# One attention and expert kernel: part of the feature map and the row scaling go to GpSimd, masks are added by quarters of the array, and the first x is transposed at other units

## The chip, the cores and the metric

The kernel runs on 1 core of one Trainium2 chip. The metric is device time in microseconds of one execution. Engines are named as in the profile: PE is TensorE (PEld its weight loads), DVE is VectorE, ACT is ScalarE, POOL is GpSimd, SP is SyncE, which issues the DMAs.

## What is computed

Three layers follow one another: attention with a memory over 4 batches and 8 heads of 576 tokens with 64 features, then a dense gated layer over the 2304 tokens, then a layer of 8 experts of which each token takes one. The change touches the first, and the normalization ahead of the second:

```python
scores = np.where(causal, -1000000000.0, scale * (q @ k.T))
a = np.exp(scores - scores.max(-1)); a /= a.sum(-1) + 1e-09
local = a @ v
phi = lambda x: np.where(x > 0, x, np.exp(x) - 1.0) + 1.0
mem_out = (phi(q) @ M_prev) / (phi(q) @ z_prev + 1e-06)
x = g * mem_out + (1 - g) * local            # 2304 tokens x 512
xn = x / np.sqrt(np.mean(x * x, -1) + 1e-06) * rms_g
y = (silu(xn @ w_gate) * (xn @ w_val)) @ w_out
```

## The kernel before

**Attention.** Two batches lie on the two halves of the 128 partitions, so one pass serves a head of both: 16 passes, called heads here. A head is five units (`ORDER`): four `Pair`s of two query tiles each, with 128, 384, 256 and 512 keys, and a `Last` for the 64 tokens left over, with 576 keys. The loop at the end of `attention` runs over 80 units and three more, and is a pipeline written out by hand: at unit u the PE computes the scores of unit u, transposes the weights of unit u-2 and multiplies those of unit u-3 with the values; ACT takes the exponentials in between. Work on the side is written as generators, each of which goes one step further at the end of a unit: `phi` (feature map of q for two heads), `load`, `rms`, the decoder's pieces of the dense weights (float64 to float32), and what `side` adds. In this part the instructions of each engine stand exactly in the order in which the program writes them (`Core.chain`), and every engine works its queue in that order. One unit takes some 2.7 us.

**Feature map** (`phi`, L248 to L261). For `phi` of two heads, one unit after another: min(q, 0) on DVE (L257), the exponential on ACT (L259), then max(q, 0) plus it, in one DVE instruction (L261). `recall` multiplies the result with the memory at the next units.

**Masks** (L336 and L382). A query tile of 64 rows for one batch and the same for the other make 128 rows; the scores come as four matmuls of 64 x 64 quarters of the array, two for each of two tiles. The causal mask is then added by one more matmul for each tile over the whole array, identity times a table of zeros and -1e9 in bf16.

**Scaling** (`rms`, L456). When the 9 tiles of a pair of batches (128 tokens x 512) are ready, ACT sums their squares, one tile a unit; POOL and DVE make y, the inverse root; then DVE multiplies each tile by its y in place (L478) and SP stores it to `xd` in DRAM. The first pair does this in the second half of attention, the other (`late`) in the first dense block.

**First x.** `xload` reads 4 tiles of `xd` back at unit (12, 2), and `xtrans` transposes a quarter of their features at each of the units in `XT` (L36, in the form (head, place in the head)) and splits it into a high and a low part: PE to PSUM (`tp`), ACT (`xh`), DVE (`xl`). The PSUM tile `tp` has the tag `m`, of which there is one buffer; `recall`'s `mp` and the `avl` of each `Last` use the same one. `avl` is written three units after its `Last`, so at units 72 and 77 for the heads 13 and 14.

**Dense layer.** Five blocks of tokens (4, 4, 4, 4 and 2 tiles), each with 12 steps f: gate and value matmuls (`gv`), tanh and products (`th`), and the output matmuls (`acc`) of the step before. Weights are kept as a high and a low part. In the first block ACT, DVE and POOL also make these parts (`Wf`), decode the last 15 pieces of weights (L206 to L219), and work off `late`. Here a scheduler orders each engine's instructions by its own model of time. The low part `sl` of the gated product is subtracted on POOL (L1014).

The expert layer behind it is not touched.

Of the kernel before, what the change touches and what calls it, by code (L numbers as in the profile page):

```python
# [12 lines left out]
AF = mybir.ActivationFunctionType  # L13
ALU = mybir.AluOpType
# [3 lines left out]
P = 128  # L18
# [14 lines left out]
FLATE = 7  # L33
DEC = [round(3 + 3.5 * k) for k in range(3 * FLATE)]
AHEAD = 3
XL, XT = (12, 2), ((14, 0), (14, 2), (14, 4), (15, 1))  # L36
NEARLY = 4
NMAIN = 18
NSLOT = 21
# [182 lines left out]
def attention(ctx, nc, tc, ins, c, g8, rp, ps, xd, side):  # L222
# [10 lines left out]
    def half(t, p):  # L233
        return p ^ (t & 1)

    def rows(p):
        return slice(64 * p, 64 * p + 64)
# [10 lines left out]
    def phi(n):  # L248

        q = pl.tile([P, 2, S], F32, tag='qs', name='q')  # L250
        nc.sync.dma_start(q, qs[n // 4, n % 4].rearrange('b p s -> p b s'))
        ph = pl.tile([P, 2, S], F32, tag='ph', name='ph')
        phis.append(ph)
        yield
        if n:
            yield
        nc.vector.tensor_scalar(ph, q, 0.0, None, op0=ALU.min)  # L257
        yield
        nc.scalar.activation(ph, ph, AF.Exp)  # L259
        yield  # L260
        nc.vector.scalar_tensor_tensor(ph, q, 0.0, ph, op0=ALU.max, op1=ALU.add)  # L261

    def values(n):

# [13 lines left out]
    for _ in load(0):  # L278
        pass
    work = [phi(0), load(1)]  # L280
    for w in work:
        next(w)
# [39 lines left out]
    class Pair:  # L322
# [5 lines left out]
        def score(self):  # L328
            H, i, w = self.H, self.i, self.w
            sc = ps.tile([P, 2, 512], F32, tag='sc', bufs=2, name='sc')  # L330
            for j in range(2):
                for p in range(2):
                    t, r = 2 * i + j, rows(half(j, p))
                    PE.matmul(sc[rows(p), j, :w], H.qt[r, 0, 64 * t:64 * t + 64], H.qt[r, 1, :w], start=True, stop=False)
            for j in range(2):
                PE.matmul(sc[:, j, i * P:w], c['identb'], c['maskb'][:, j], start=False, stop=True)  # L336
            m = sm.tile([P, 2], F32, tag='m', name='m')
            nc.vector.tensor_reduce(m, sc[:, :, :w], axis=AX.X, op=ALU.max, negate=True)
            self.sc, self.m = sc, m
# [28 lines left out]
    class Last:  # L368
# [5 lines left out]
        def score(self):  # L374
            H = self.H
            m = sm.tile([P, 2], F32, tag='m', name='m')
            sc = ps.tile([P, 2, 512], F32, tag='sc', bufs=2, name='scl')
            for u in range(2):
                for p in range(2):
                    r = rows(p)  # L380
                    PE.matmul(sc[r, u, :288], H.qt[r, 0, 512:576], H.qt[r, 1, 288 * u:288 * u + 288], start=True, stop=(u == 0))
            PE.matmul(sc[:, 1, 224:288], c['identb'], c['maskb'][:, 0, :64], start=False, stop=True)  # L382
            mx = sm.tile([P, 2], F32, tag='mx', name='mx')
            nc.vector.tensor_reduce(mx, sc[:, :, :288], axis=AX.X, op=ALU.max, negate=True)
            nc.vector.tensor_tensor(m[:, 0:1], mx[:, 0:1], mx[:, 1:2], op=ALU.min)
            self.sc, self.m = sc, m
# [17 lines left out]
        def value(self):  # L404
            H = self.H
            avl = ps.tile([P, 64], F32, tag='m', name='avl')
            for k in range(5):
                for p in range(2):
                    lt, rhs = (self.aT[:, k], H.v[:, H.h, k, p]) if k < 4 else (self.aT[:64, 4], H.vL[:, H.h, p])
                    PE.matmul(avl[rows(p)], lt[:, rows(p)], rhs, start=(k == 0), stop=(k == 4))  # L410
            add(H, avl)
            if H.hh == 7 and H.bp == 0:
                work.append(rms(0))
# [42 lines left out]
    def rms(bp, ps=None):  # L456

        ts, n = (0, 1, 2, 3, 8, 4, 5, 6, 7), 9
        x = [xs[bp][t // 4][:, t % 4] for t in ts]
        pool = rp if bp else cp  # L460
        ss, y, z = (pool.tile([P, 9], F32, tag=f'{n}{bp}', name=n) for n in ('ss', 'y', 'z'))
        if 'mhalf' not in state:
            state['mhalf'] = rp.tile([P, 9], F32, name='mhalf')
            nc.gpsimd.memset(state['mhalf'], -0.5)
        for t in range(n):
            sq = cp.tile([P, 512], F32, tag='sq', name='sq') if not bp else ps.tile([P, 512], F32, tag='m', name='sq')
            nc.scalar.activation(sq, x[t], AF.Square, accum_out=ss[:, t:t + 1])
            yield
        nc.vector.tensor_scalar(ss, ss, 1.0 / 512, 1e-6, op0=ALU.mult, op1=ALU.add)
        nc.gpsimd.tensor_tensor(y, ss, state['mhalf'], op=ALU.pow)  # L470
        yield
        yield
        nc.vector.tensor_tensor(z, y, y, op=ALU.mult)
        nc.vector.tensor_tensor(z, z, ss, op=ALU.mult)
        nc.vector.tensor_scalar(z, z, -0.5, 1.5, op0=ALU.mult, op1=ALU.add)
        nc.vector.tensor_tensor(y, y, z, op=ALU.mult)
        for j, t in enumerate(ts):
            nc.vector.tensor_scalar(x[j], x[j], y[:, j:j + 1], None, op0=ALU.mult)  # L478
            r = (8 * bp + t if t < 8 else 16 + bp) * P
            nc.sync.dma_start(xd[r:r + P, :], x[j])  # L480
            yield
# [4 lines left out]
    for u in range(5 * 16 + LAG2):  # L486
        n, j = u // 5, u % 5
        if n < 16:
            if j == 0:
                H = start(n)  # L490
            if j == LD and n < 14:
                work.append(load(n + 2))
            if u % 10 == 1 and n < 14:
                work.append(phi(n // 2 + 1))
            if u == 32:
                memory(1)
            if u % 10 == 4 and n < 14:
                values(n // 2 + 1)
            units.append(Last(H) if ORDER[j] == 4 else Pair(H, ORDER[j]))
            units[u].score()  # L500
# [21 lines left out]
    def late(ps):  # L522
        yield from rms(1, ps)
# [586 lines left out]
PE = None  # L1110
# [98 lines left out]
```

## Time and profile before

| | us |
|---|---|
| time, median of 3 runs (lowest to highest) | 1040.76 (1039.47 to 1041.92) |
| the profiled execution's own time | 1039.59 |
| its span, first to last instruction | 1037.9 |
| PE busy in it (mean granted clock 0.991) | 974.7 |
| DVE busy | 696.3 |
| ACT busy | 569.8 |
| POOL busy | 248.8 |

A span is the time from the first to the last instruction of the profiled execution; 1.7 us of that execution lie around it. Attention runs from 0 to about 236 us, the first dense block from there to about 346, the other four to about 730, the experts behind them to the end. An engine's busy share says little by itself; what a change in a stage is worth is read from the waits and the chain there.

### The profile page before, as it was taken

The numbers are of one execution on the slowest core, as the hardware profiler recorded it, in microseconds if no ns is written. First come the engines' busy times: TensorE is split into PE (matmuls) and PEld (weight loads), VectorE is DVE, ScalarE is ACT, GpSimd is POOL, SyncE is SP. The second block draws the span as 40 slices with busy tenths as digits, with TensorE's granted clock in tenths as the row PEclk, the third lists the DMA queues.
The fourth block names the chain that finished last, engine by engine and source line by source line (L and its number), as shares of the span: only waits on it lengthen the run. The fifth ranks groups of instructions, "written<-read, shape, count | busy, mean of one in ns | idle before, by whom it ended". The sixth has DMA issues, their size and how long they took to land.

```text
span 1037.9 us, 18552 instructions
## 1 busy us (share of the span) xinstructions
PE 974.7 (94%) x6727; PEld 752.1 (72%) x6727; DVE 696.3 (67%) x1256; ACT 569.8 (55%) x1113; POOL 248.8 (24%) x241
## 2 busy tenths in 40 slices
PE   7999989799899999999999999999989999999995
PEld 4666656557676768887888778878768888777784
DVE  6788899777986544334422462357688889888884
ACT  6888887766343322222222222244557888888884
POOL 1233243235454311110111112123012121222110
PEclk9999999989999999999999999999999999999999
DMA  9466557315644311121211112144124552396332
GB/s 313 152 206 188 181 168 229 107 62 179 208 131 142 112 31 62 32 73 29 72 32 51 31 63 65 35 162 134 41 83 143 172 197 76 122 339 216 102 112 89
DMA packets 51278, 128.20 MB, mean 124 GB/s; under 512 B 9965, under 2 KB 10477, under 8 KB 50672
## 3 DMA queue, kind: packets, MB, share of 16 engines
q1 hardware_dynamic: 47664, 116.48, 34.9%
q0 software_dynamic: 3520, 10.51, 3.2%
q8 instruction: 54, 0.88, 0.4%
q14 instruction: 40, 0.33, 0.1%
HBM read 160.50 MB, written 22.04 MB: 176 GB/s over the span
## 4 chain that ended last, share of the span: by engine, by line
PE 60%; DVE 14%; issue 8%; DMA 7%; ACT 7%; POOL 2%; SPq 0%; ACTq 0%; POOLq 0%; DVEq 0%
PE gv L56 22%; PE acc L56 11%; PE y L56 9%; PE h L56 7%; DMA out_dram<-ys,to 2%; DVE m L56 2%; PE av L56 2%; PE sc L56 2%; PE tr L56 2%; DMA wo<-woutd 1%; PE tp L56 1%; ACT whl L858 1%; PE htp L56 1%; DVE whl L859 1%; DVE dt L56 1%
## 5 line engine op out<-in xcount | busy, mean ns | idle before, releaser
L56 PE MATMUL gv<-xh,Wf 128*128 128x512 f32 (+1 forms) x960 | 291.2, 376 | 8.9 <-DVE th L1009 3.2
L859 DVE TENSOR_TENSOR whl<-raw,whl 128x1024 fp32r<-128x1024 f32 x173 | 204.3, 1220 | 32.0 <-ACT whl L858 31.6
L56 PEld LDWEIGHTS gv<-xh,Wf 128*128 128x128 f32 x960 | 175.7, 190 | 44.5 <-DVE th L1009 4.8
L858 ACT CAST whl<-raw 128x1024 fp32r<-128x1024 f32 x176 | 177.0, 1059 | 17.2 <-PE h L56 5.1
L56 PE MATMUL gv<-xl,Wf 128*128 128x512 f32 (+1 forms) x480 | 177.6, 370 | 0.0
L1014 POOL TENSOR_TENSOR sl<-th,sh 128x512 fp32r<-128x512 f32 (+1 forms) x58 | 73.0, 1259 | 321.5 <-ACT sh L1013 316.9
L56 PE MATMUL y<-whl,hh 128*128 128x512 f32 x528 | 138.3, 402 | 2.3 <-DVE whl L859 1.5
L56 PE MATMUL h<-whl,xgh 128*128 128x512 f32 x352 | 117.3, 401 | 2.7 <-DVE whl L859 2.0
L56 PEld LDWEIGHTS y<-whl,hh 128*128 128x128 f32 x528 | 97.5, 190 | 23.4 <-DVE whl L859 2.1
L56 PEld LDWEIGHTS gv<-xl,Wf 128*128 128x128 f32 x480 | 91.2, 190 | 14.2
L1013 ACT CAST sh<-th 128x512 fp32r<-128x512 f32 (+1 forms) x60 | 34.5, 576 | 118.9 <-DVE th L1010 118.9
L951 DVE TENSOR_TENSOR wol<-wo,woh 128x512 fp32r<-128x512 f32 x60 | 45.0, 751 | 70.3 <-ACT woh L950 70.3
L56 PE MATMUL acc<-woh,sh 128*128 128x512 f32 x216 | 86.6, 401 | 1.0 <-ACT sh L1013 0.9
L56 PE MATMUL acc<-wol,sh 128*128 128x512 f32 x216 | 85.3, 395 | 0.0
L56 ACT ACTIVATE a<-sc,m 128x128 f32<-128x128 f32 (+3 forms) x128 | 67.0, 534 | 30.5 <-DVE m L56 17.4
L1009 DVE SCALAR_TENSOR_TENSOR th<-th,gv 128x512 f32<-128x512 f32 (+1 forms) x60 | 37.9, 631 | 63.0 <-ACT th L1008 62.7
L56 PEld LDWEIGHTS h<-whl,xgh 128*128 128x128 f32 x352 | 64.6, 188 | 21.2 <-DVE whl L859 7.0
L56 PE MATMUL acc<-woh,sl 128*128 128x512 f32 x216 | 77.7, 397 | 2.2 <-POOL sl L1014 2.2
L1008 ACT ACTIVATE th<-gv 128x512 f32<-128x512 f32 (+1 forms) x60 | 33.2, 554 | 81.0 <-PE gv L56 76.9
L950 ACT CAST woh<-wo 128x512 fp32r<-128x512 f32 x60 | 37.1, 619 | 63.0 <-PE acc L56 43.3
L1010 DVE TENSOR_TENSOR th<-th,gv 128x512 f32<-128x512 f32 (+1 forms) x60 | 37.9, 632 | 49.8 <-PE gv L56 49.2
L56 PE MATMUL h<-whl,xgl 128*128 128x512 f32 x176 | 68.7, 392 | 0.0
(252 smaller groups left out, 1572.8 us busy)
## 6 DMA issues: line engine op xcount, KB each, us to landing
raw<-in_wf_dram SPq DMA_DIRECT2D x168, 512.0 KB
wo<-woutd SPq DMA_DIRECT2D x60, 256.0 KB
raw<-in_wgv_dram SPq DMA_DIRECT2D x24, 512.0 KB
qt<-in_qk_dram SPq DMA_DIRECT2D x16, 576.0 KB
raw<-in_wout_dram SPq DMA_DIRECT2D x12, 512.0 KB
q<-in_qs_dram SPq DMA_DIRECT2D x8, 576.0 KB
xd<-x SPq DMA_DIRECT2D x18, 256.0 KB
rowd<-xr SPq DMA_DIRECT2D x4, 1028.0 KB
```

Of the source, the lines that this page charges most:

```text
L56: i = call(*args, **kw).ins
L858: nc.scalar.copy(w[:, 0], src)
L859: (nc.gpsimd if k in pool_k else nc.vector).tensor_tensor(w[:, 1], src, w[:, 0].bitcast(F32), op=ALU.subtract)
L950: nc.scalar.copy(woh, wo)
L951: nc.vector.tensor_tensor(wol, wo, woh.bitcast(F32), op=ALU.subtract)
L1008: nc.scalar.activation(th, g[0], AF.Tanh, scale=0.5)
L1009: nc.vector.scalar_tensor_tensor(th, th, 1.0, g[0], op0=ALU.add, op1=ALU.mult)
L1010: nc.vector.tensor_tensor(th, th, g[1], op=ALU.mult)
L1013: nc.scalar.copy(sh, th)
L1014: (nc.vector if f >= 10 and bi == last else nc.gpsimd).tensor_tensor(sl, th, sh.bitcast(F32), op=ALU.subtract)
```

## The change

There are four edits. In `phi` the minimum on DVE goes; ACT takes the exponential of q itself, one unit earlier than before; POOL takes max(q, 0) in place, one unit later; DVE then forms min(exp(q), 1) + max(q, 0), where it stood before. In the masks each whole-array matmul becomes two, of the quarters that the scores used. In `rms` the multiplication of a tile by y goes from DVE to POOL. In `XT` the second and the fourth place change.

```diff
--- before.py
+++ after.py
@@ -33,7 +33,7 @@
 FLATE = 7
 DEC = [round(3 + 3.5 * k) for k in range(3 * FLATE)]
 AHEAD = 3
-XL, XT = (12, 2), ((14, 0), (14, 2), (14, 4), (15, 1))
+XL, XT = (12, 2), ((14, 0), (14, 3), (14, 4), (15, 0))
 NEARLY = 4
 NMAIN = 18
 NSLOT = 21
@@ -254,11 +254,11 @@
         yield
         if n:
             yield
-        nc.vector.tensor_scalar(ph, q, 0.0, None, op0=ALU.min)
-        yield
-        nc.scalar.activation(ph, ph, AF.Exp)
-        yield
-        nc.vector.scalar_tensor_tensor(ph, q, 0.0, ph, op0=ALU.max, op1=ALU.add)
+        nc.scalar.activation(ph, q, AF.Exp)
+        yield
+        nc.gpsimd.tensor_scalar(q, q, 0.0, None, op0=ALU.max)
+        yield
+        nc.vector.scalar_tensor_tensor(ph, ph, 1.0, q, op0=ALU.min, op1=ALU.add)
 
     def values(n):
 
@@ -333,7 +333,9 @@
                     t, r = 2 * i + j, rows(half(j, p))
                     PE.matmul(sc[rows(p), j, :w], H.qt[r, 0, 64 * t:64 * t + 64], H.qt[r, 1, :w], start=True, stop=False)
             for j in range(2):
-                PE.matmul(sc[:, j, i * P:w], c['identb'], c['maskb'][:, j], start=False, stop=True)
+                for p in range(2):
+                    r = rows(half(j, p))
+                    PE.matmul(sc[rows(p), j, i * P:w], c['identb'][r, r], c['maskb'][r, j], start=False, stop=True)
             m = sm.tile([P, 2], F32, tag='m', name='m')
             nc.vector.tensor_reduce(m, sc[:, :, :w], axis=AX.X, op=ALU.max, negate=True)
             self.sc, self.m = sc, m
@@ -379,7 +381,9 @@
                 for p in range(2):
                     r = rows(p)
                     PE.matmul(sc[r, u, :288], H.qt[r, 0, 512:576], H.qt[r, 1, 288 * u:288 * u + 288], start=True, stop=(u == 0))
-            PE.matmul(sc[:, 1, 224:288], c['identb'], c['maskb'][:, 0, :64], start=False, stop=True)
+            for p in range(2):
+                r = rows(p)
+                PE.matmul(sc[r, 1, 224:288], c['identb'][r, r], c['maskb'][r, 0, :64], start=False, stop=True)
             mx = sm.tile([P, 2], F32, tag='mx', name='mx')
             nc.vector.tensor_reduce(mx, sc[:, :, :288], axis=AX.X, op=ALU.max, negate=True)
             nc.vector.tensor_tensor(m[:, 0:1], mx[:, 0:1], mx[:, 1:2], op=ALU.min)
@@ -475,7 +479,7 @@
         nc.vector.tensor_scalar(z, z, -0.5, 1.5, op0=ALU.mult, op1=ALU.add)
         nc.vector.tensor_tensor(y, y, z, op=ALU.mult)
         for j, t in enumerate(ts):
-            nc.vector.tensor_scalar(x[j], x[j], y[:, j:j + 1], None, op0=ALU.mult)
+            nc.gpsimd.tensor_scalar(x[j], x[j], y[:, j:j + 1], None, op0=ALU.mult)
             r = (8 * bp + t if t < 8 else 16 + bp) * P
             nc.sync.dma_start(xd[r:r + P, :], x[j])
             yield
```

In the order of the instructions the change shows at three places that matter.

ScalarE around one feature map (here the one for the heads 12 and 13), before; `a` are the softmax weights, `aT` their transposes, `aL` and `scl` those of a `Last`, `ph` the feature map:

```order
L56 COPY aT<-tr 128x384 x2
L56 ACTIVATE a,sums<-sc,m 128x512 x2
L56 COPY aT<-tr 128x2x256
L56 ACTIVATE aL,sums<-scl,m 128x288 x2
L56 ACTIVATE qt<-qt 128x576
L56 ACTIVATE ph<-ph 128x1152
```

and after:

```order
L56 COPY aT<-tr 128x384 x2
L56 ACTIVATE a,sums<-sc,m 128x512 x2
L56 ACTIVATE ph<-q 128x1152
L56 COPY aT<-tr 128x2x256
L56 ACTIVATE aL,sums<-scl,m 128x288 x2
L56 ACTIVATE qt<-qt 128x576
```

The exponential moved ahead of a copy, the weights of the `Last` and the scaling of the next head's q.

TensorE at the second transposition of x, before (`avl` is the product of head 13's `Last` with the values, into the buffer that `tp` takes next):

```order
L56 MATMUL avl<-v,aTL 64x64 x8
L56 MATMUL avl<-vL,aTL 64x64 x2
L56 MATMUL tp<-ident,xt 128x128 x4
L56 MATMUL sc<-qt 64x512 x4
```

and after, where the masks by quarters show as well:

```order
L56 MATMUL avl<-v,aTL 64x64 x8
L56 MATMUL avl<-vL,aTL 64x64 x2
L56 MATMUL sc<-qt 64x512 x4
L56 LDWEIGHTS identb
L56 MATMUL sc<-maskb,identb 64x128
L56 LDWEIGHTS identb
L56 MATMUL sc<-maskb,identb 64x128
L56 LDWEIGHTS identb
L56 MATMUL sc<-maskb,identb 64x128
L56 LDWEIGHTS identb
L56 MATMUL sc<-maskb,identb 64x128
L56 MATMUL tr<-ident,a 128x128 x6
```

A unit's scores, masks, transposes and products now lie between `avl` and `tp`; on the other hand the second, third and fourth `tp` follow one another at a distance of one unit.

GpSimd in the first dense block, before (from `y` of the second pair of batches on; `sl` is the low part of the gated product, `Wf` low parts of weights, `sq` the decoder's last addition):

```order
L56 TENSOR_TENSOR y<-ss,mhalf 128x9
L1014 TENSOR_TENSOR sl<-th,sh 128x512
L211 TENSOR_TENSOR sq<-dt,sq 128x512
L219 TENSOR_TENSOR Wf<-sq,Wf 128x512
L56 TENSOR_TENSOR Wf<-dw,Wf 128x512
L1014 TENSOR_TENSOR sl<-th,sh 128x512
```

and after:

```order
L56 TENSOR_TENSOR y<-ss,mhalf 128x9
L1018 TENSOR_TENSOR sl<-th,sh 128x512
L211 TENSOR_TENSOR sq<-dt,sq 128x512
L56 TENSOR_SCALAR x_1717<-x_1717,y 128x512 x4
L56 TENSOR_SCALAR x_1719<-x_1719,y 128x512
L56 TENSOR_SCALAR x_1718<-x_1718,y 128x512 x4
L219 TENSOR_TENSOR Wf<-sq,Wf 128x512
L56 TENSOR_TENSOR Wf<-dw,Wf 128x512
L211 TENSOR_TENSOR sq<-dt,sq 128x512
L1018 TENSOR_TENSOR sl<-th,sh 128x512
```

All nine scalings stand in one piece ahead of the weights of step 3.

## Rows read from the trace of the kernel before

**Rows 1.** Stretches, core 0: start:end, us, busy us (instructions) per engine, clock, DMA share, GB/s

```profile
0.00:236.00 236.00, 210.48 (x3089) 138.78 (x3089) 191.06 (x402) 178.20 (x522) 69.30 (x108) 0.99 0.56 178
236.00:276.00 40.00, 36.86 (x160) 28.98 (x161) 33.04 (x52) 20.61 (x43) 21.04 (x16) 1.00 0.65 214
346.00:690.00 344.00, 338.87 (x1581) 273.29 (x1580) 136.24 (x310) 92.98 (x163) 53.75 (x44) 1.00 0.18 54
```

**Rows 2.** Chain that ended last: shares by engine and line, 0 to 236 and 236 to 276

```profile
by line: issue 8.7%; DVE m L56 8.5%; PE av L56 8.2%; PE sc L56 7.8%; PE tr L56 7.1%; DVE dt L56 4.4%; ACT a L56 4.4%; PE mp L56 4.1%; ACT aL L56 4.1%; ACT aT L56 3.9%; DVE sq L56 3.8%; DVE tm L56 3.6%; DVE r L56 2.9%; ACT ph L56 2.8%; DMA q
...
by line: DMA dw<-wgvd 18.5%; DMA wo<-woutd 16.8%; DVE x L56 13.1%; DVE Wf L56 10.7%; issue 7.4%; DVE z L56 6.2%; DVE wol L951 5.1%; POOL x L56 4.3%; POOL sl L1014 3.4%; DVE th L1010 3.0%; SPq L196 2.1%; DVE dt L208 2.0%; DVE Wf L219 1.7%; D
```

**Rows 3.** Timeline, TensorE around the x transposes: start us, us, engine, line, instruction

```profile
10.69 1.09 PE L56 MATMUL sc<-qt 64*64 64x512 f32 x8 [0.79 <-ACT a L56]
...
207.87 1.11 PE L56 MATMUL tp<-ident,xt 128*128 128x128 f32 x4 [2.68 <-DVE tm L56]
208.92 1.99 PE L56 MATMUL sc<-qt 64*64 64x512 f32 x8
...
223.89 0.69 PE L56 MATMUL avl<-v,aTL 128*64 128x64 f32 x16 [1.64 <-DVE xl L56]
...
224.78 1.92 PE L56 MATMUL sc<-qt 64*64 64x512 f32 x6
```

**Rows 4.** Stretches of 2 and 1 us after the two waits, columns as in rows 1

```profile
208.00:210.00 2.00, 2.00 (x12) 0.89 (x12) 0.25 (x1) 0.97 (x2) 1.39 (x3) 0.50 0.00 0
225.00:226.00 1.00, 1.00 (x8) 0.01 (x2) 0.93 (x4) 0.89 (x4) 0.00 (x0) 0.50 0.91 352
```

**Rows 5.** Timeline, TensorE: masks and the transposes behind them

```profile
112.01 0.29 PE L56 MATMUL sc<-maskb,identb 128*128 128x128 bf16 x2
112.13 1.04 PE L56 MATMUL tr<-ident,a 128*128 128x128 f32 x8
```

**Rows 6.** Tile ph: duration ns min/median/max, first and last start

```profile
L56 DVE TENSOR_SCALAR ph<-q x8: 746/748/1825, 6.9 to 180.0; 128x1152 f32<-128x1152 f32 x8
```

**Rows 7.** Waits from 0 to 228: us in total, times, longest

```profile
DVE ph L56 <- ACT ph L56: 8.8, 7, 1.9
```

**Rows 8.** Chain in order of time, 92 to 104: start us, us, what

```profile
98.87 1.05 ACT ph L56
```

**Rows 9.** Tile x: the scaling by mean square, duration ns min/median/max

```profile
L56 DVE TENSOR_SCALAR x<-x,y x18: 471/478/1508, 151.1 to 262.6; 128x512 f32<-128x512 f32 x18
```

**Rows 10.** Groups of instructions by line: busy us, mean ns

```profile
L56 POOL MEMSET MZ<- 128x1040 f32 x1 | 1.0, 964 | 0.1
```

**Rows 11.** Tile dt of the decoder: duration ns min/median/max

```profile
L56 DVE TENSOR_SCALAR dt<-sq x21: 412/419/986, 27.3 to 227.3; 128x512 int32<-128x512 int32 x21
L56 DVE SCALAR_TENSOR_TENSOR dt<-raw,dt x21: 672/683/1439, 30.2 to 229.4; 128x512 int32<-128x512 int32 x21
...
L56 POOL TENSOR_TENSOR sq<-dt,sq x21: 1262/1280/1733, 34.9 to 232.3; 128x512 f32<-128x512 f32 x21
```

**Rows 12.** Stretch 0 to 236, instructions that touch dt alone (VectorE, then GpSimd)

```profile
0.00:236.00 236.00, 40.71 (x63) 27.71 (x21) 0.99 0.56 178
```

**Rows 13.** Timeline, 210.3 to 212: a GpSimd and a VectorE instruction side by side

```profile
210.30 1.27 POOL L56 TENSOR_TENSOR Wf<-dw,Wf 128x512 fp32r<-128x512 f32 x1 [0.91 <-ACT Wf L56]
210.41 1.45 DVE L56 TENSOR_SCALAR sq<-dt 128x512 int32<-128x512 int32 x1
```

**Rows 14.** Timeline, first dense block, 257 to 267

```profile
257.03 4.12 DVE L56 TENSOR_SCALAR x<-x,y 128x512 f32<-128x512 f32 x5
259.06 1.42 POOL L56 TENSOR_TENSOR Wf<-dw,Wf 128x512 fp32r<-128x512 f32 x1
260.53 0.73 PE L56 MATMUL gv<-xh,Wf 128*128 128x512 f32 x2 [0.76 <-POOL Wf L56]
265.86 0.73 PE L56 MATMUL gv<-xh,Wf 128*128 128x512 f32 x2 [1.07 <-DVE Wf L56]
```


## The prediction

> **What bounds the kernel now.** I read the stretches first, then the chain of waits, then single waits and timelines. In the stretches [rows 1] PE is busy 338.9 of 344 us in the dense blocks behind the first, where nothing of this change runs: whatever is won or lost ahead of 346 us is carried through them to the end. In attention PE is busy 210.5 of 236 us, DVE 191.1, ACT 178.2, POOL 69.3; no engine alone is the bound. The chain [rows 2] says how they share it: between 0 and 236 us the first five PE entries (products, scores, transposes) have 27%, DVE's maxima, decoder steps and small factors about as much, ACT's exponentials and copies most of the rest. So an edit in attention is worth the part of its engine time that falls where that engine is on the chain, some 40% for PE and 50% for DVE by these shares. From 236 to 276 us the chain is DMA and DVE, with the scaling of x alone (DVE x) at 13.1% of 40 us, 5.2 us.
>
> **The change, part by part.** Terms are summed against the profiled execution's 1039.6 us, which is 1.2 us below the median.
>
> *x transposes.* The second `tp` waits 2.68 us for DVE to read `avl`, and the `avl` at unit 77 waits 1.64 us for DVE's `xl` of the fourth `tp`, one unit before [rows 3]. Behind both waits the granted clock is 0.50, which is 1.2 instead of 2.4 GHz [rows 4], and the scores of 512 keys take 1.99 and 1.92 us instead of 1.09 [rows 3]: 0.90 + 0.83 us more. Together 6.0 us of PE. The change puts a unit (some 2.7 us) between `avl` and the second `tp`, and two between the fourth and the next `avl`, which covers both waits. What is late next: the second, third and fourth `tp` are now one unit apart and share one buffer, as fourth `tp` and `avl` did, which cost 1.64 us. For each of the two new neighbours I take 1 us between 0 and 1.64, without a drop of the clock. 6.0 - 2.0 = 4.0 us of PE, of which I count 60%, since each of these stalls stops DVE too: **-2.5** (bounds -6.0, and 0 if both new waits are full and the clock falls again).
>
> *Masks.* 64 units have two masks of 128 columns, 16 have one of 64; the transposes begin 0.12 us after the masks [rows 5]. By quarters, two masks run in different quarters at the same time, so half of this time can go: 0.06 x 64 = 3.8 us of PE, 40% of it on the chain: **-1.5**. No row shows a bf16 matmul in a quarter. Below: all 0.12 hidden behind the scores, 7.7 us of PE, -3. Above: nothing overlaps, and four instead of two run at the same length, 0.12 x 64 = 7.7 us more, +3.
>
> *Feature map.* Eight minima leave DVE, 0.75 us each [rows 6], 6.0 us, and with those that were held up some 7; half of it on the chain: -3.5. Then, DVE stood waiting for ACT's exponential seven times, 8.8 us in all, 1.26 each [rows 7]. The exponential now runs one unit, 2.7 us, earlier, and POOL's maximum of M us stands between it and DVE: DVE's wait becomes 1.26 - 2.7 + 0.1 + M, so zero up to M = 1.3. Most of this wait is not the chain's: ACT's own 1.05 us of exponential are [rows 8], and these move into time in which ACT waited for a maximum. I take 1 us. Together **-4.5** (bounds 0 and -11).
>
> *Scaling, in attention.* Nine multiplications of 0.48 us [rows 9] leave DVE, 4.3 us, where DVE is on the chain more than before: **-3.5** (bounds -2 and -4.3). The stores wait for POOL instead; the load of x is five units and more behind the scalings it needs, so that wait is covered, and without this cover would be one POOL instruction.
>
> *What GpSimd takes.* The trace shows no such instruction on POOL. The nearest below is its memset, which only writes: 964 ns for 1040 columns [rows 10], so 0.47 us for 512 columns and 1.07 for 1152. The nearest above is its addition of two inputs, 1.28 us for 512 columns [rows 11], so 2.9 for 1152. One input lies between them, and I take D = 0.75 us for 512 columns and M = 1.5 for 1152: nearer the memset, as one stream of input is missing. In attention POOL is idle 70% of the time, so its own 8 x 1.5 + 9 x 0.75 = 18.8 us are beside other work.
>
> *What this does to VectorE.* POOL holds DVE up: a `tensor_scalar` that takes 0.42 us [rows 11] took 1.45, beginning 0.11 us after a POOL subtraction of 1.27 us and ending 0.29 us behind its end [rows 13]. The decoder's 63 DVE instructions took 40.7 us [rows 12] where 42 x 0.42 + 21 x 0.68 = 31.9 were due [rows 11]: 8.8 us lost beside 69.3 us of POOL, 0.13 for each us of POOL; with the other DVE instructions I take 0.2. 18.8 x 0.2 = 3.8 us, mostly on the chain: **+3** (bounds +1.5 and +8). The Trainium skill (SBUF — State Buffer, Who interferes with whom) says more sharply that the pair of ports which both engines share is an exclusive lock: the one that starts first has it for its whole instruction, and the other blocks fully. The pair of instructions above agrees with that; what the rule would make of the whole sum is a rival below.
>
> *First dense block.* DVE loses 5.8 us of scaling, 5.2 of them on the chain, and PE's idle 3.1 us between 236 and 276 us [rows 1] are all there is to win. But POOL has the nine scalings in one piece ahead of the weights of step 3. In the trace they could start at 257.0, where DVE's did; POOL ended that step's `Wf` at 260.5 and PE waited 0.76 us for it [rows 14]. Now 257.0 + 9 x 0.75 + 1.5 for DVE's instructions in between + 1.4 + 1.4 for the two `Wf` = 268.1, 7.6 us later. The new order of PE covers 4.6 of it: 12 matmuls of the step's other half and 8 of `acc` at 0.23 us stand ahead of the first that needs it. That leaves a stall of 3.0 us, and the waits of 3.1 us that go balance it: **0** (bounds -3 and, at D = 1.28, +5). Behind it POOL has half its time free and catches up.
>
> Sum: -2.5 - 1.5 - 4.5 - 3.5 + 3 + 0 = **-9.0**. From 1039.6 this is 1030.6; with the 1.2 us by which the median lies higher, **1031.8 us**.
>
> **Rivals.**
> - *Slower: GpSimd's scaling is slow.* If a multiplication by a column of factors costs POOL more than its two-input addition, the place that decides is the piece of nine in the first dense block: each 0.1 us of D moves `Wf` by 0.9 us, costs DVE 0.1 us x 27 of POOL x 0.2 = 0.5 us in attention, and lets DVE's last step of the feature map wait 0.2 us more, eight times, half of it felt. That is 2.2 us for each 0.1 us from about D = 1.0 on; with -9.0 at 0.75 and some -6 at 1.0, the gain is gone at D = 1.3. At 1.6 it would be 7 us above: 1047. For it: nothing shows the instruction. Against it: it reads one tensor, not two. Chance 0.11.
> - *Slower: the ports.* If DVE stood still for all of POOL's new 18.8 us and not for a fifth, the sum would be -9.0 + 15.8 = +6.8, so 1047.6. The exclusive lock of the Trainium skill's page on SBUF would do this if all of DVE's instructions needed the shared pair. Against it: the measured 0.13 for each us; maxima from PSUM do not slow down. Chance 0.04.
> - *No difference.* The stalls of the transposes move by a unit (0), masks gain nothing (0), feature map and scaling give 2 us each, VectorE loses 3: -1, so 1039.8. For it: in attention three engines are close to each other, and the chain changes hands within each unit. Chance 0.12.
> - *More.* Every term at or near its favourable end (the feature map, whose end is far off, at -6): -6 - 3 - 6 - 4 + 2 - 1 = -18: 1022.8. Chance 0.13.
>
> **How the numbers follow.** My forecast, with its terms within half their bounds, runs from 1026 to 1037 and has 0.60. Eight in ten need more on both sides: up to 1041, which takes in no difference, and down to 1024, which takes in half of *more*; outside are the two slower cases (0.15) and the rest. 0.2% of this kernel, 2.1 us, is about what a measurement can tell from no change. Faster by more: 0.60 + 0.13 = 0.73; within: 0.12; slower: 0.15.
>
> **What would show it.** Right: the waits of PE for DVE `tm` and `xl` above 1.5 us gone and the clock at 1.00 around 210 and 225 us; the wait of DVE `ph` for ACT gone, with none for POOL above 0.3 us; the masks' transposes 0.06 us behind them; attention ending near 226 us and the first dense block as long as before, 110 us. Wrong: a POOL scaling above 1.2 us, PE waiting for POOL's `Wf` by more than 4 us near 255 us, the decoder's DVE instructions above 44 us in attention, or attention ending after 234 us.

## The result and the profile after

The changed kernel takes 1047.12 us (median of 5 runs, 1044.72 to 1047.59); the kernel before took 1040.76. The ratio is 1.006 with a 95% interval from 1.0046 to 1.0074: 0.6% slower, some 6 us, where 1031.8 was forecast and the range ended at 1041. The profiled execution took 1047.59 us, 8.0 more than that of before, and its profile tells where they are.

The stretches of the changed kernel (columns as in [rows 1]):

```profile
0.00:236.00 236.00, 207.73 (x3192) 143.38 (x3194) 188.70 (x383) 177.39 (x521) 110.69 (x124) 0.99 0.55 177
236.00:276.00 40.00, 31.63 (x170) 23.93 (x166) 21.75 (x37) 17.90 (x40) 28.14 (x19) 0.96 0.57 185
...
346.00:690.00 344.00, 338.86 (x1559) 272.52 (x1558) 136.99 (x311) 91.29 (x159) 57.64 (x46) 1.00 0.16 52
```

TensorE is busy 207.7 us in attention and 31.6 of 40 us behind it, for 210.5 and 36.9 before; from 346 to 690 us it is as busy as before. Two rows fix the ends of the stages: the last product of attention, and the first transposition for the experts' router, which before comes some 13 us behind the 346 us at which the first dense block ends (instructions, ns min/median/max, first and last start). Before:

```profile
L56 PE MATMUL avl<-vL,aTL x64: 218/267/363, 26.1 to 235.3; 64*64 64x64 f32 x64
```

```profile
L56 PE MATMUL tp<-ident,xr x72: 270/272/330, 359.0 to 751.0; 128*128 128x128 f32 x72
```

and after:

```profile
L56 PE MATMUL avl<-vL,aTL x64: 218/267/366, 26.0 to 237.3; 64*64 64x64 f32 x64
```

```profile
L56 PE MATMUL tp<-ident,xr x72: 270/272/330, 369.2 to 760.7; 128*128 128x128 f32 x72
```

Attention ends at 237.3 us for 235.3, 2.0 later; from there to the router's first transposes it takes 131.9 us for 123.7. So 8.2 of the 10.2 us that are lost up to here lie in the first dense block, which was forecast at no difference, and attention lost 2 where 9 were to be won. The two executions differ by 8.0 us in all, so 2.2 us come back behind the first of these transposes. That stretch, which the change does not touch, took 675.5 to 679.7 us in the profiled executions of this document, so a stage of a single execution can differ by some 2 us to either side without cause in the change.

The two new kinds of GpSimd instruction, each in the view of its tile:

```profile
L56 POOL TENSOR_SCALAR x<-x,y x18: 1558/1699/2762, 153.3 to 273.5; 128x512 f32<-128x512 f32 x18
```

```profile
L56 POOL TENSOR_SCALAR q<-q x8: 3120/3178/3463, 8.9 to 184.6; 128x1152 f32<-128x1152 f32 x8
```

1.70 us for a scaling (forecast: 0.75) and 3.18 for a maximum (forecast: 1.5): more than twice, and more than the addition of two inputs [rows 11]. Nine in one piece follow one another at 1.68 us, as the timeline of GpSimd in the first dense block shows, with the weights that stand behind them:

```profile
259.98 15.11 POOL L56 TENSOR_SCALAR x<-x,y 128x512 f32<-128x512 f32 x9 [0.33 <-DVE y L56]
275.07 1.26 POOL L219 TENSOR_TENSOR Wf<-sq,Wf 128x512 fp32r<-128x512 f32 x1
276.29 1.27 POOL L56 TENSOR_TENSOR Wf<-dw,Wf 128x512 fp32r<-128x512 f32 x1
```

TensorE beside it:

```profile
268.27 0.40 PE L56 MATMUL acc<-wol,sh 128*128 128x512 f32 x1
274.34 0.79 PE L56 MATMUL gv<-xh,Wf 128*128 128x512 f32 x1 [5.67 <-ACT Wf L56]
...
277.62 1.22 PE L56 MATMUL gv<-xh,Wf 128*128 128x512 f32 x2 [2.06 <-POOL Wf L56]
```

It is through at 268.7 us with all that it has, then waits 5.67 us for ScalarE's high part of the weights and, after two matmuls, 2.06 us for GpSimd's low part, which is ready at 277.6. Behind such a stop TensorE runs slowly; the same holds for the transposes of x in attention, where a stretch shows it too (granted clock third from the right: 0.66 and 0.50; 0.50 is 1.2 instead of 2.4 GHz):

```profile
220.00:225.00 5.00, 4.52 (x49) 3.07 (x51) 3.48 (x7) 2.81 (x10) 0.00 (x0) 0.66 0.51 163
...
276.00:280.00 4.00, 2.38 (x6) 1.90 (x7) 1.91 (x2) 0.66 (x1) 4.00 (x5) 0.50 0.45 161
```

The waits in attention (us in total, times, longest) answer to [rows 7] and [rows 3]:

```profile
DVE ph L56 <- POOL q L56: 13.6, 4, 4.6
PE mp L56 <- DVE ph L56: 5.4, 6, 2.6
PE tp L56 <- DVE xl L56: 4.1, 2, 3.3
```

VectorE's 8.8 us of waiting for ScalarE's exponential are gone, and 13.6 us for GpSimd's maximum have come; TensorE waits 5.4 us behind that, and 4.1 us at two transposes of x for the 2.68 and 1.64 us of before.

### The profile page after: what moved, and what is told of

The parts are those of the page before. It is cut to its first block, busy times and chain, and to the rows that moved or that the text cites. A ratio compares the mean times of both kernels' runs of the same rounds, so it can differ in the third digit from the quotient of the medians.

```text
span 1045.8 us, 18843 instructions
## 1 busy us (share of the span) xinstructions
PE 975.8 (93%) x6871; PEld 760.2 (73%) x6871; DVE 690.3 (66%) x1230; ACT 569.5 (54%) x1113; POOL 306.1 (29%) x267
## 4 chain that ended last, share of the span: by engine, by line
PE 63%; DVE 13%; issue 8%; DMA 6%; POOL 5%; ACT 4%; SPq 0%; POOLq 0%; ACTq 0%; DVEq 0%
PE gv L56 22%; PE acc L56 12%; PE y L56 8%; PE h L56 7%; PE tr L56 3%; PE av L56 2%; PE sc L56 2%; DMA out_dram<-ys,to 2%; POOL x L56 2%; DVE m L56 1%; PE mp L56 1%; DVE whl L863 1%; PE tp L56 1%; ACT whl L862 1%; DMA raw<-in_wf_dram 1%
## 5 line engine op out<-in xcount | busy, mean ns | idle before, releaser
L56 PE MATMUL gv<-xh,Wf 128*128 128x512 f32 (+1 forms) x960 | 290.9, 376 | 13.6 <-ACT Wf L56 6.3
L929 POOL DMA_INDIRECT out_dram<-ys,to x22 | 31.7, 1439 | 129.9 <-ACT ys L928 68.0
```

The costliest lines, as they stand in the source:

```text
L56: i = call(*args, **kw).ins
L929: nc.gpsimd.indirect_dma_start(self.out, idx(to), ys, None, bounds_check=NTOK - 1, oob_is_err=False)
```

## The experiments

Ratios are to the kernel before, run beside it on the same chip, with 95% intervals; 0.1% is 1.04 us. Stage lengths come from the one profiled execution of each.

### One edit alone: the scaling, in both places and in attention only

```diff
-            nc.vector.tensor_scalar(x[j], x[j], y[:, j:j + 1], None, op0=ALU.mult)
+            nc.gpsimd.tensor_scalar(x[j], x[j], y[:, j:j + 1], None, op0=ALU.mult)
```

> Only the scaling by mean square goes to GpSimd, in attention and in the first dense block. Theory A (the instruction's price: 1.7 us each, and nine in one piece ahead of the weights of step 3): attention ends within 1.5 us of 236, PE waits 5 to 8 us for weights between 262 and 280 us, the first dense block is 7 to 9 us longer, the whole 1046 to 1049 us. Theory B (the ports: VectorE held up by GpSimd): attention ends 3 us later or more, the first dense block is at most 3 us longer, 1045 us. The prediction's step (0.75 us each): 1037 to 1038 us.

Measured: 1046.9 us, 1.0045 (1.0028 to 1.0062), as theory A had it, with a first dense block longer still than its 7 to 9 us (below). For attention only, `(nc.vector if bp else nc.gpsimd)` stands in that line:

> Only the nine scalings of the first pair of batches go to GpSimd; those in the first dense block stay on VectorE. Theory A: the first dense block is as before, attention is within 1.5 us of before, the whole 1039.5 to 1042 us. Theory B: 9 x 1.7 = 15.3 us more of GpSimd hold VectorE for about half of that, less the 4.3 us it is freed of: attention 3 to 4 us longer, 1044 us.

Measured: 1037.9 us, 0.9969 (0.9956 to 0.9982). In attention the scaling on GpSimd wins 3.2 us; in the first dense block it loses 0.45 + 0.31 = 0.76%, 7.9 us. Theory B (VectorE held up by GpSimd for half of 15 us) has the wrong sign in attention; theory A, with 1039.5 to 1042 us, expected no gain there. The timeline of the first run, GpSimd and then TensorE in the first dense block, repeats that of the changed kernel:

```profile
258.87 15.22 POOL L56 TENSOR_SCALAR x<-x,y 128x512 f32<-128x512 f32 x9 [1.01 <-DVE y L56]
...
273.34 0.80 PE L56 MATMUL gv<-xh,Wf 128*128 128x512 f32 x1 [5.79 <-ACT Wf L56]
...
276.61 1.22 PE L56 MATMUL gv<-xh,Wf 128*128 128x512 f32 x2 [2.05 <-POOL Wf L56]
```

From the last product of attention to the router's transposes this run took 133.5 us, the other 123.3, and the kernel before 123.7: 10.2 us between the two by these single executions, 7.9 by the times.

That the piece of nine lies on the chain that ends last can be read from the changed kernel's trace (255 to 290 us, shares by engine and line; `POOL x` has the nine, 37.0% of 35 us):

```profile
by line: POOL x L56 37.0%; issue 10.2%; DVE dt L208 8.8%; POOL sq L211 7.3%; DVE z L56 7.1%; DVE wol L955 6.6%; DVE Wf L56 5.6%; DVE dt L207 4.4%; POOL Wf L219 3.6%; POOL Wf L56 3.5%; DVE xl L56 2.1%; DVE sq L210 2.0%; DVE sq L209 1.9%; DVE
```

### Which queue makes the first dense block wait

The load of step 3's `dw` stands on SyncE's queue behind stores of x that wait for GpSimd's scaling; ScalarE's wait could come from there. In this run only the second pair is scaled on GpSimd, and GpSimd issues its stores:

```diff
+            (nc.gpsimd if bp else nc.vector).tensor_scalar(x[j], x[j], y[:, j:j + 1], None, op0=ALU.mult)
+            (nc.gpsimd if bp else nc.sync).dma_start(xd[r:r + P, :], x[j])
```

> Only the nine scalings in the first dense block go to GpSimd, and their stores are issued by GpSimd instead of SyncE, so that no load of weights stands behind a store that waits. Theory A1 (GpSimd's own piece of nine ahead of the weights of step 3 decides): TensorE waits for GpSimd's Wf until 276 us or later, the first dense block is 7 us longer or more, the whole 1048 us or more. Theory A2 (SyncE's queue decides: the load of dw stands behind stores that wait for GpSimd, and ScalarE's Wf waits for it, 5.7 us of TensorE): that wait goes below 1.5 us and the first dense block is at most 4 us longer, 1045 us or less. Both together: the wait for ScalarE goes, and one for GpSimd of the same end comes in its place.

Measured: 1057.5 us, 1.0176 (1.0157 to 1.0195).

```profile
257.05 14.77 POOL L56 TENSOR_SCALAR x<-x,y 128x512 f32<-128x512 f32 x9 [0.34 <-DVE y L56]
...
270.03 0.80 PE L56 MATMUL gv<-xh,Wf 128*128 128x512 f32 x1 [4.29 <-ACT Wf L56]
...
275.17 1.22 PE L56 MATMUL gv<-xh,Wf 128*128 128x512 f32 x2 [3.92 <-POOL Wf L56]
```

TensorE's wait for ScalarE is still 4.29 us with SyncE's queue free of these stores, and the one for GpSimd grew to 3.92 us: it ends 18.1 us after the piece began, as in the run before (276.61 - 258.87 = 17.7). (A1 had the end at 276 us or later; it came at 275.2, as the piece began earlier.) ScalarE's part comes 13.0 us after the piece's beginning for 14.5. SyncE's queue does not make this difference. The load `dw` takes one of the two buffers that the load `wo` uses too, and SyncE issues it as soon as VectorE has read the `wo` before it: VectorE's `wol` ended at 269.59 us in the run of the scaling in both places, and SyncE issued `dw` at 269.61. In this run the one ended at 266.86, and the other shows on SyncE's timeline:

```profile
266.89 8.56 SPq L559 DMA_DIRECT2D dw<-wgvd  x2
```

So ScalarE's wait is that of two loads, one after the other through the same buffers; in this run they landed sooner (4.1 and 2.5 us after their issue for 5.2 and 3.1). Behind it GpSimd's low part is late anyway: GpSimd's piece decides, not SyncE's queue. What makes this run still slower, 18 us above the kernel before, was not separated; in its profiled execution the first dense block is 136.3 us long for 133.5, and the stores themselves take GpSimd 0.5 to 0.8 us each.

### The same scaling at another price

```diff
+            nc.gpsimd.tensor_tensor(x[j], x[j], y[:, j:j + 1].broadcast_to([P, 512]), op=ALU.mult)
```

> The scaling on GpSimd, in attention and in the first dense block, with the factor as a second input that is repeated over the 512 columns, so a multiplication of two inputs instead of one by a column of scalars. If the price is that of the form (two inputs took 1.28 us in the trace of before): 1.26 to 1.3 us each, the piece of nine ends 2.5 us earlier than with 1.56 us, the whole 2 to 3 us below the scaling by a scalar: 1044 us. If a repeated input is dearer: 1.6 us or more each and 1047 us or more.

Measured: 1042.4 us, 1.0031 (1.0014 to 1.0047), so 1.4 us below the scaling by a scalar, with overlapping intervals. The tile x, then GpSimd's timeline and TensorE's:

```profile
L56 POOL TENSOR_TENSOR x<-x,y x18: 1034/1223/2152, 153.3 to 268.6; 128x512 f32<-128x512 f32 x18
...
258.83 10.84 POOL L56 TENSOR_TENSOR x<-x,y 128x512 f32<-128x512 f32 x9 [0.32 <-DVE y L56]
...
272.67 0.74 PE L56 MATMUL gv<-xh,Wf 128*128 128x512 f32 x2 [0.40 <-POOL Wf L56]
```

A median of 1.22 us for 1.56: the form with two inputs is the cheaper one. The piece takes 10.84 us for 15.22, and the first dense block 127.2 us for 133.5. Price and length of the block move together, as the first rival had it. Of these 6.3 us attention, which ends 2.1 us later in this execution, takes a part back, and the ratios of the two runs, taken on two chips, differ by 1.4 us only; the 2 to 3 us that were expected are within their intervals.

### One edit alone: the feature map, and where its maximum is taken

```diff
-        nc.vector.tensor_scalar(ph, q, 0.0, None, op0=ALU.min)
-        yield
-        nc.scalar.activation(ph, ph, AF.Exp)
-        yield
-        nc.vector.scalar_tensor_tensor(ph, q, 0.0, ph, op0=ALU.max, op1=ALU.add)
+        nc.scalar.activation(ph, q, AF.Exp)
+        yield
+        nc.gpsimd.tensor_scalar(q, q, 0.0, None, op0=ALU.max)
+        yield
+        nc.vector.scalar_tensor_tensor(ph, ph, 1.0, q, op0=ALU.min, op1=ALU.add)
```

> Only the feature map changes. Theory A (GpSimd's maximum takes 3.2 us and comes between ScalarE and VectorE): VectorE waits for it some 10 us in four places or more, PE 3 to 6 us, and what the earlier exponential wins is given back: attention 0 to 2 us longer, 1041 to 1043 us. Theory B: 25 us more of GpSimd, VectorE held for half of it, less the 7 us it is freed of: attention 4 us longer or more, 1045 us. The prediction's step: 1036 us.

Measured: 1043.7 us, 1.0025 (1.001 to 1.0041), between the two theories' times. Attention ends at 238.8 us, 3.5 later than before, and VectorE waits 9.0 us for the maximum, in three places (shown below). Next, the same with `nc.vector` for `nc.gpsimd`:

> The feature map with the exponential a unit earlier as in the change, but max(q, 0) stays on VectorE, where the minimum's 0.75 us was: GpSimd's order of work is that of before. If GpSimd's 3.2 us alone are what turns the feature map's gain into a loss: VectorE's wait for ScalarE's exponential (8.8 us in 7 places) is gone and 1 to 3 us are won, 1038.5 to 1040.5 where before has 1041.5. If the early exponential itself costs (it delays a softmax of ScalarE, which VectorE and TensorE wait for): 0 to 2 us slower than before, as slow as with GpSimd.

Measured: 1035.0 us, 0.9963 (0.9949 to 0.9977). VectorE does as much work here as before and 3.9 us are won; so the win, more than the 1 to 3 us expected, is that of the earlier exponential, whose wait has shrunk from 8.8 us to this:

```profile
DVE q L56 <- ACT ph L56: 2.2, 3, 0.8
```

and GpSimd's maximum costs 0.62%, 6.5 us (between two runs on two chips, each against the kernel before). Is that VectorE waiting for the maximum, or VectorE held up while GpSimd takes it? The third variant gives the maximum a buffer of its own and a unit more:

```diff
+        mx = pl.tile([P, 2, S], F32, tag='qr', bufs=1, name='mx')
         nc.scalar.activation(ph, q, AF.Exp)
+        nc.gpsimd.tensor_scalar(mx, q, 0.0, None, op0=ALU.max)
         yield
         yield
+        nc.vector.scalar_tensor_tensor(ph, ph, 1.0, mx, op0=ALU.min, op1=ALU.add)
```

> The feature map with max(q, 0) on GpSimd as in the change, but into a buffer of its own, so that it starts in the unit of the exponential, beside it, and VectorE takes both one unit later than that, where it did before. If the loss of the feature map on GpSimd comes from VectorE's wait for the late maximum (9.0 us in three places in the run with the feature map alone, TensorE's wait behind it): that wait falls below 2 us and the time is that of the variant with the maximum on VectorE or better, 0.4% below before. If it comes from GpSimd holding VectorE at the ports for 25 us: VectorE's decoder instructions of 3 us stay and the time is as with the feature map alone, 0 to 0.3% above before.

Measured: 1041.1 us, 1.0009 (0.9996 to 1.0022). With the feature map alone the waits were

```profile
DVE ph L56 <- POOL q L56: 9.0, 3, 3.0
```

and here that for GpSimd is gone. In its place (0 to 236 us, the instructions on the decoder's tile `dt`, VectorE's busy us and then GpSimd's; first the run with the maximum on VectorE, then that with the feature map alone, then this one):

```profile
0.00:236.00 236.00, 41.88 (x63) 30.23 (x21) 0.99 0.56 181
```

```profile
0.00:236.00 236.00, 46.46 (x63) 27.14 (x21) 0.99 0.56 177
```

```profile
0.00:236.00 236.00, 55.45 (x63) 29.27 (x21) 0.98 0.55 177
```

The decoder's 63 instructions on VectorE take 9.0 us more than with the feature map alone, just what the wait took. One of them, which takes 0.42 us when clean [rows 11], beside the maximum:

```profile
44.57 3.12 POOL L56 TENSOR_SCALAR mx<-q 128x1152 f32<-128x1152 f32 x1
44.87 3.11 DVE L56 TENSOR_SCALAR dt<-sq 128x512 int32<-128x512 int32 x1 [0.23 <-ACT sq L56]
...
48.83 1.34 DVE L56 SCALAR_TENSOR_TENSOR ph<-ph,mx 128x1152 f32<-128x1152 f32 x1
```

It ends 0.29 us after GpSimd's does, and the feature map's last step comes at 48.83. So the wait went, as the first expectation had it, and the time stayed high, as the second had it. Against the maximum on VectorE, the feature map alone loses 46.46 - 41.88 + 9.0 = 13.6 us of VectorE in the decoder and the wait, and this run 55.45 - 41.88 = 13.6 in the decoder alone: where GpSimd's maximum stood chose only whether VectorE loses them in a wait or in a blocked instruction. Whether the 1.7 us between the two times are real stays open, as their intervals overlap.

### One edit alone: the units of the transposes, and the masks

```diff
+XL, XT = (12, 2), ((14, 0), (14, 3), (14, 4), (15, 0))
```

> Only the units of x's transposes change. The prediction's step: the waits of 2.68 and 1.64 us go, two of at most 1.64 us come, no clock below 0.9: 1038 us. Theory C (the third and fourth transposes wait 0.8 and 3.3 us for VectorE in their stead, and the clock falls behind the longer one, as in the changed kernel): attention within 1 us of before, 1040 to 1041 us.

Measured: 1042.3 us, 1.0006 (0.9992 to 1.002). The stalls pass on: TensorE waits 0.81 and 3.26 us for `xl` at the third and fourth transpose, for 2.68 and 1.64 us before. Attention ends 2.8 us later than before in the one profiled execution, where theory C had at most 1. What each `tp` has to pass first, ScalarE's `xh` and behind it VectorE's `xl`, has not become shorter (VectorE's wait, before and then here):

```profile
DVE xl L56 <- ACT xh L56: 8.4, 4, 2.7
```

```profile
DVE xl L56 <- ACT xh L56: 8.2, 4, 2.7
```

The masks by quarters:

```diff
-                PE.matmul(sc[:, j, i * P:w], c['identb'], c['maskb'][:, j], start=False, stop=True)
+                for p in range(2):
+                    r = rows(half(j, p))
+                    PE.matmul(sc[rows(p), j, i * P:w], c['identb'][r, r], c['maskb'][r, j], start=False, stop=True)
...
-            PE.matmul(sc[:, 1, 224:288], c['identb'], c['maskb'][:, 0, :64], start=False, stop=True)
+            for p in range(2):
+                r = rows(p)
+                PE.matmul(sc[r, 1, 224:288], c['identb'][r, r], c['maskb'][r, 0, :64], start=False, stop=True)
```

> Only the masks go by quarters of the array. The prediction's step: 3.8 us of TensorE saved, 40% of it felt: 1.5 us below the kernel before of this call. What is left over when the parts measured so far (scaling +4.7, feature map +2.6, transposes +0.6) are taken from the whole (+6.2): also about 1.5 us below. Rival (the chain in attention is with VectorE and ScalarE, so TensorE's 0.06 us a unit are not felt): within 0.7 us of before.

Measured: 1040.3 us, 1.0005 (0.9991 to 1.0018). One unit on TensorE, before and then in this run:

```profile
111.63 0.45 PE L56 MATMUL sc<-qt 64*64 64x128 f32 x8
112.01 0.29 PE L56 MATMUL sc<-maskb,identb 128*128 128x128 bf16 x2
112.13 1.04 PE L56 MATMUL tr<-ident,a 128*128 128x128 f32 x8
```

```profile
111.73 0.45 PE L56 MATMUL sc<-qt 64*64 64x128 f32 x8
112.00 0.24 PE L56 MATMUL sc<-maskb,identb 64*64 64x128 bf16 x4
112.17 1.09 PE L56 MATMUL tr<-ident,a 128*128 128x128 f32 x8
```

The masks start 0.27 instead of 0.38 us behind the first score, but the transposes 0.17 instead of 0.12 behind them: from score to transposes 0.44 us for 0.50. The transposes wait longer behind the four masks than behind the two, so the half that was to go by overlap did not go; TensorE wins the 0.06 us a unit at another place than forecast, and the time does not show it.

### What won, together

The exponential early with the maximum on VectorE, and the first pair's scaling on GpSimd, the second's on VectorE:

```diff
+        nc.scalar.activation(ph, q, AF.Exp)
+        yield
+        nc.vector.tensor_scalar(q, q, 0.0, None, op0=ALU.max)
...
+            (nc.vector if bp else nc.gpsimd).tensor_scalar(x[j], x[j], y[:, j:j + 1], None, op0=ALU.mult)
```

> The two parts that won alone: the exponential a unit earlier with the maximum on VectorE (-0.37%), and the first pair's scaling on GpSimd, the second's on VectorE (-0.31%). If both are felt in the same chain of VectorE: -0.5 to -0.7%, 1033 to 1036 us where before has 1041; if GpSimd's 14 us hold VectorE more once it is the bound less: -0.4%.

Measured: 1032.0 us, 0.9929 (0.9908 to 0.9949): faster than either kernel, 7.4 us below the one before. In its profile attention ends at 229.7 us, 5.6 earlier, and the first dense block takes 123.4 us. The next run adds the two diffs of the section above to it.

> The same with the masks by quarters and the new units of the transposes, that is the change with the maximum and the second pair's scaling back on VectorE. Alone neither moved the time (+0.05 and +0.06%). If they are not felt: within 0.15% of the kernel without them in this call. If they are felt once VectorE is freed: 1 to 3 us below it.

Measured: 1035.5 us, 0.995 (0.9933 to 0.9967), neither of the two expected: 0.2% above the kernel without them. To see which of the two edits costs, each was put on alone, first the line of `XT`:

> The two winning parts and the new units of the transposes. If the stall only passes on (0.81 and 3.26 us for 2.68 and 1.64): within 0.15% of the kernel of the winning parts, which in the last call stood at 0.9929 of before. If it costs: most of the 3.6 us, 0.995 of before or more. The prediction's step would be 2.5 us below, 0.9905.

Measured: 1034.7 us, 0.9936 (0.9918 to 0.9954). Then the masks:

> The two winning parts and the masks by quarters. If the masks are neutral: 0.993 of before. If they cost (twice the instructions on TensorE's queue, no time won between the scores and the transposes): 0.995 or more.

Measured: 1031.6 us, 0.9919 (0.9892 to 0.9945). Neither can be told from the kernel of the winning parts (0.9929), so neither edit by itself costs or wins anything that these runs can show; whether both together cost 0.2% stays open, as the intervals overlap. Another spacing of the transposes, on the winning parts:

```diff
+XL, XT = (12, 2), ((14, 0), (14, 4), (15, 0), (15, 4))
```

> The two winning parts, with the second transpose at the place that was the third's, the third right behind it at the next head's first place, and the last at that head's last place. If spacing takes the stalls away: no wait of TensorE for tm of 2.68 us, one for the third of 0.8 to 3.3 us, the last without: 1 to 3 us below the kernel of the winning parts, 0.990 to 0.992 of before. If the last one is now too late for the first dense block: its first matmuls wait 1 us or more, 0.993 or above.

Measured: 1031.7 us, 0.9921 (0.9896 to 0.9946).

```profile
210.77 0.66 PE L56 MATMUL tp<-ident,xt 128*128 128x128 f32 x4 [2.73 <-DVE xl L56]
...
229.97 0.50 PE L56 MATMUL gv<-xh,Wf 128*128 128x512 f32 x1 [1.44 <-DVE tm L56]
```

One stall of 2.73 us instead of two, and 1.44 for 0.39 us at the first dense matmul: the time cannot be told from that of the winning parts, so again nothing won. Last, the second pair's scaling on ScalarE:

```diff
+            if bp:
+                nc.scalar.mul(x[j], x[j], y[:, j:j + 1])
+            else:
+                nc.gpsimd.tensor_scalar(x[j], x[j], y[:, j:j + 1], None, op0=ALU.mult)
```

> As the one that takes the two winning parts, with the second pair's scaling on ScalarE (nine of about 0.6 us, in two pieces). In the first dense block ScalarE is busy half of the time and VectorE 83%. If VectorE's 5.2 us on the chain there were a loss: 1 to 3 us below that kernel. If TensorE's weights through ScalarE become late instead: 0 to 3 us above it.

Measured: 1035.3 us, 0.9951 (0.9934 to 0.9969). ScalarE's high part of the weights is late in GpSimd's stead: TensorE waits 6.22 us for it at 258.95, as the second expectation had it. The 2.3 us to the kernel of the winning parts are within the intervals.

## Why the prediction was wrong, step by step

**What GpSimd takes.** This step failed, and what the scaling in the first dense block and the feature map lost follows from it; the transposes and the masks failed by steps of their own. I set 0.75 and 1.5 us as "nearer the memset, as one stream of input is missing". Measured are 1.56 to 1.70 and 3.18 (medians): beyond the upper bound, which I took from the addition. The signs of "wrong" came with it: GpSimd's scaling above 1.2 us, the decoder at 47.9, attention's end at 237.3, and TensorE's stop of 5.67 + 2.06 us ahead of GpSimd's `Wf`. The Trainium skill (GPSIMD Engine Reference, 4.1 Engine selection) has one-input work on GpSimd at roughly line rate and two-input work about twice as slow; here the one-input scaling took 1.56 us and the two-input one 1.22, and the measurement decides.

**First dense block: 0 forecast, 7.9 us lost** (runs of the scaling in both places and in attention only). The mechanism and the place were named; the price was mis-sized. From the start of the piece in the changed kernel, 15.1 us for the nine and 2.5 for the two `Wf` give 259.98 + 17.6 = 277.6, and TensorE went on at 277.62. Of the 9.5 us by which this is later than the 268.1 of the prediction, 8.4 are the price and 3.0 the later start of the piece; the 1.5 us put down for VectorE's instructions in between did not come. Not in the sum was the clock of 0.50 behind the stop. The first rival, 1047 us at 1.6 us a scaling, is what came, at a chance of 0.11: its price was put down as unlikely by the same argument. The second rival, the ports, names nearly the same time, but it puts the loss into attention, where the profile shows only 2.0 us of it.

**Feature map: -4.5 forecast, less a port share of 2.4; +2.6 measured** (1.0 to 4.3). 1 us of this was for the earlier exponential, 3.5 for the minima that leave VectorE. The first was too small: with as many instructions on VectorE as before, the earlier exponential alone wins 3.9. The second has the wrong sign: the maximum on GpSimd loses 6.5 against one on VectorE. VectorE's wait was to be "zero up to M = 1.3"; M is 3.18, and VectorE waits 3.4 us in each of four places where it waited 1.26 in seven.

**What this does to VectorE.** The decoder's instructions take 47.93 us in the changed kernel for 40.71 [rows 12]:

```profile
0.00:236.00 236.00, 47.93 (x63) 27.14 (x21) 0.99 0.55 177
```

7.2 us beside 41.4 us more of GpSimd, 0.17 for each, near the 0.2 I took; the term of +3 had 18.8 us of GpSimd in it where 41.4 came. That the share came out near is luck: it is no property of the engines. By the same views it was (55.45 - 40.71) / 26.4 = 0.56 where the maximum ran beside the decoder, and (41.90 - 40.71) / 16.9 = 0.07 for the scalings of the first pair. In single instructions the exclusive lock of the Trainium skill (SBUF — State Buffer, Who interferes with whom) shows in full, in the changed kernel with 3.14 us for 0.42:

```profile
184.57 3.12 POOL L56 TENSOR_SCALAR q<-q 128x1152 f32<-128x1152 f32 x1 [0.62 <-DVE dt L56]
184.83 3.14 DVE L56 TENSOR_SCALAR sq<-dt 128x512 int32<-128x512 int32 x1
```

**Scaling in attention: -3.5 forecast, less a port share of 1.4; -3.2 measured** (-4.6 to -1.9). Right, though each scaling took twice what I had and the port share came out smaller: in that run no wait of TensorE or VectorE for a scaled x shows in attention.

**Transposes: -2.5 forecast, +0.6 measured** (-0.8 to +2.1). "For each of the two new neighbours I take 1 us between 0 and 1.64, without a drop of the clock" failed: the fourth waited 3.28 us for VectorE's `xl` of the third, and the clock fell to 0.66 behind it:

```profile
214.47 0.66 PE L56 MATMUL tp<-ident,xt 128*128 128x128 f32 x4 [0.81 <-DVE xl L56]
...
220.48 0.66 PE L56 MATMUL tp<-ident,xt 128*128 128x128 f32 x4 [3.28 <-DVE xl L56]
```

At each of the spacings tried, TensorE met the chain from `tp` over ScalarE's `xh` to VectorE's `xl` at another place, and the stall moved with it; which part of that chain would have to become shorter was not tried.

**Masks: -1.5 forecast, +0.5 measured** (-0.9 to +1.9). Half of the masks' time was to go by overlap; 0.06 us a unit went, at their start, so the size is right by luck; that 40% of it would be felt failed. (The 27% of the chain named for TensorE are four of its entries [rows 2], not five.)

The parts measured alone add up to 7.9 + 2.6 - 3.2 + 0.6 + 0.5 = +8.4 us, each with an interval of about 1.4 to either side, the sum with some 3; the whole is +6.2, so the parts account for it within the noise.

## What to carry to other kernels

Before work goes to GpSimd, measure the very instruction there, in its form and size; its own additions and fills do not bound it. Then look at what stands behind it on GpSimd's queue: nine scalings whose results nobody waited for won 3.2 us, as VectorE was relieved of them; the same nine ahead of a weight that TensorE needs cost 7.9 us. And a long GpSimd instruction beside VectorE's work in SBUF can cost VectorE all of its length, as a wait or as a blocked instruction (from 0.07 to 0.56 us for each us of GpSimd in these runs); giving the maximum a unit more did not win that back here.

## What the runs showed of the hardware that was not expected

On GpSimd a multiplication of 512 columns by a column of scalars takes 1.55 us at least, and the same with the factor repeated as a second input 1.03 to 1.22. VectorE took 0.48 [rows 9], and ScalarE 0.70 (the run with ScalarE). Four matmuls of 64 x 64 quarters with 128 bf16 columns held the next whole-array transposes up 0.05 us more than two matmuls of the whole array did, though they started 0.11 us earlier behind the scores.
